# A two-stage linear-attention and gated-MLP layer: reversed layernorm rows on VectorE, contiguous KV copies, reciprocals on either engine, split last tile, new instruction order

## The chip, the cores and the metric

One NeuronCore of a Trainium2 chip. The metric is the device time in microseconds (us) of one execution, the median of several runs. The four runs of the kernel before lie within 0.2% of each other. The five engines run side by side (in the kernel before, TensorE is busy 277.9, VectorE 173.9, ScalarE 154.2 and GpSimd 90.3 us of the same 298.1) and meet at semaphores: TensorE (PE in the profile; its weight loads are PEld), VectorE (DVE), ScalarE (ACT), GpSimd (POOL) and the queue that starts DMA transfers (SP).

## The reference

Input x is 2048 rows of 640 bf16 values. There are two residual stages.

```python
h  = x + A(layernorm(x))          # 32 heads of 20, linear attention
# A: q, k, v = x @ wqkv;  phi(t) = [softmax(t @ w_phi), softmax(-t @ w_phi)]   (per head)
#    kv = phi_k^T v;  z = sum(phi_k);  o = (phi_q kv) / (phi_q z + 1e-6);  return o @ wo
h2 = h + B(layernorm(h))          # B: ((y @ w_gate) * (y @ w_up)) @ w_down,  640 -> 1536 -> 640
```

What matters is the shape of the dependences. Every key row must be projected, exponentiated, summed per head, divided and multiplied into `kv` before the first numerator `phi_q kv` can start. Everything after that can be streamed.

## The kernel before

The kernel records its operations as units and lets a small list scheduler in the same file place them: each unit has a priority (one number per unit, in a list called `ORDER`), a cost, and sometimes a choice of engines (`alts`). The scheduler walks through time and gives each free engine the ready unit of best priority. So a change in one operation's cost or choice of engine can move every instruction of the kernel.

The first stage, per tile of 128 rows: layernorm statistics on VectorE, the normalised row written on ScalarE, a DMA transpose, the V and K projections on TensorE, two exponentials on ScalarE, a sum per head and its reciprocal on VectorE, a multiply on GpSimd, and an accumulation of `kv` on TensorE. The parts that the change touches:

```python
def ln_apply(t, dst):                                   # layernorm row, first stage
    k = xn_p.new()
    R.add("scalar", lambda e: e.activation(out=real(k), in_=x_all[:, t, :], func=ACT.Identity,
                                           bias=mv[:, t, 4:5], scale=mv[:, t, 3:4]), ..., cost=0.92)
    return dma(dst, k, 163840, tr=True)                 # transpose into xnT[:, t, c, :]

def normalise(v, n):                                    # softmax of a key tile, after its exponentials
    sr = sr_p.new()
    R.add("vector", ... tensor_reduce(out=sr[:, 0:n], in_=v, op=ALU.add) ...)
    R.add("vector", ... reciprocal(out=sr[:, 66:66 + n], in_=sr[:, 0:n]) ..., cost=0.56)
    tt("gpsimd", v, v, sr[:, 66:66 + n].unsqueeze(2).to_broadcast([P, n, DH]), ALU.mult)

def kv_evac(c, n):                                      # kv from PSUM to SBUF, masked by g
    ...
    tt("vector", KV[0:kr, c:c + n, HG:HG + DH * nh].rearrange("p c (d h) -> p c h d", d=DH), psv[:, :, :, 0:DH],
       g.unsqueeze(3).to_broadcast([kr, n, nh, DH]), ALU.mult)

def watt(t):                                            # attention output of a tile, second layernorm
    ...
    R.add("scalar", ... activation(out=real(k), in_=h, func=ACT.Identity, bias=nm) ..., cost=0.83,
          alts=[("vector", ... tensor_scalar(out=real(k), in0=h, scalar1=nm, op0=ALU.add) ..., 0.55)])

def fd(t):                                              # last projection of a tile and its store
    pr = psum.new(2)
    ...                                                 # 12 x (512 + 128 columns) of matmul
    R.add("vector", ... scalar_tensor_tensor(out=real(k), in0=real(pr)[:, 0:D], scalar=r2, in1=h, ...) ..., cost=0.88)
    dma(out[0, P * t:P * (t + 1), :], k, 163840, writes=[])
```

The KV copy writes head by head, `d` innermost. In the destination `h` is innermost with six heads, so each element is written six elements (12 bytes) after the last.

The softmax here doesn't subtract the row's maximum and nothing guards it: scores larger than these inputs give would overflow.

## Time and profile before

| | before |
|---|---|
| time, median of 4 runs (range) | 300.24 us (299.85 to 300.54) |
| span of the profiled run | 298.1 us |
| TensorE busy | 277.9 us, 93% |
| first denominator matmul starts | 89.72 us |
| from there to the end | 208.4 us |

The engine line of the page gives busy time, share of the span and number of instructions of each engine.

```profile
...
PE 277.9 (93%) x1969; PEld 163.1 (55%) x2006; DVE 173.9 (58%) x307; ACT 154.2 (52%) x339; POOL 90.3 (30%) x66
...
```

TensorE is the bound: 277.9 of 298.1 us. (37 of its 2006 matmuls are missing from this trace, 1969 against 2006 weight loads; each leaves a false gap of some 0.05 us, 2.0 us in all. Without these gaps TensorE's busy time would be about 279.8.)

The table by stretches cuts the span into pieces. Its columns are the stretch and its length, then busy us and number of instructions of PE, PEld, DVE, ACT and POOL, then the granted TensorE clock as a share of full speed, the busy share of the DMA engines and GB/s.

```profile
...
0.00:20.00 20.00, 13.56 (x110) 9.71 (x113) 14.10 (x35) 13.93 (x25) 14.33 (x34) 1.00 0.73 195
20.00:40.00 20.00, 17.97 (x166) 11.47 (x167) 17.44 (x33) 16.45 (x31) 12.68 (x6) 1.00 0.85 137
40.00:60.00 20.00, 19.79 (x172) 12.31 (x174) 17.17 (x29) 16.53 (x34) 15.47 (x7) 1.00 0.81 181
60.00:80.00 20.00, 17.22 (x155) 10.98 (x157) 15.54 (x19) 13.94 (x28) 18.53 (x8) 1.00 0.84 205
80.00:100.00 20.00, 16.39 (x159) 10.02 (x159) 19.45 (x38) 10.05 (x30) 12.38 (x7) 1.00 0.76 164
...
```

TensorE's idle time is what is left of each 20 us: 6.4, 2.0, 0.2, 2.8 and 3.6 us. Much of the first is the wait for weights (5.3 us, for the DMA of `wqkv`). Between 20 and 80 us VectorE and ScalarE are busy 14 to 17 of 20 us, and GpSimd 18.5 in the last stretch.

The timeline lists instructions in order of time: start, duration, engine, line, operation, output<-input, count, and in brackets the engine's idle time just before, with what ended it.

```profile
...
22.48 2.36 POOL L645 TENSOR_TENSOR r<-r,sr 128x1280 bf16<-128x1280 bf16 x1 [6.26 <-DVE sr L787]
...
81.44 2.36 POOL L645 TENSOR_TENSOR r<-r,sr 128x1280 bf16<-128x1280 bf16 x1 [1.07 <-DVE sr L821]
...
85.89 1.81 DVE L645 TENSOR_TENSOR KV<-ps,G 120x480 bf16<-120x480 f32 x1 [0.55 <-PE ps L628]
...
87.42 1.91 DVE L645 TENSOR_TENSOR KV<-ps,G6d 120x480 bf16<-120x480 f32 x1
...
89.40 0.39 PE L628 MATMUL ps<-pqT,KV 128*128 128x256 bf16 x2 [1.74 <-DVE Zd L891]
...
89.72 1.05 PE L628 MATMUL ps<-pqT,Zd 120*32 120x256 bf16 x22
...
99.97 2.42 POOL L645 TENSOR_TENSOR phq<-phq,sr 128x1320 bf16<-128x1320 bf16 x1 [2.16 <-DVE sr L823]
...
101.13 1.45 DVE L983 TENSOR_SCALAR xn<-x_all,mv 128x640 bf16<-128x640 bf16 x1
...
```

The first key multiply of GpSimd starts at 22.48, after a wait of 6.26 us for a reciprocal of VectorE (line 787). The last one ends at 81.44 + 2.36 = 83.80. The two large KV copies come at 85.89 and 87.42 and take 1.81 and 1.91 us. TensorE waits 1.74 us for the evacuation and starts the first numerator at 89.40 and the first denominator at 89.72. The last two lines are another matter: a VectorE row write (line 983) takes 1.45 us when it starts inside a GpSimd multiply. It ends at 102.58; the multiply ends at 102.39. That row is usually short (a median of 0.386 us), as the groups by shape show (busy time, then mean ns of one, then the idle time before). VectorE:

```profile
...
L983 DVE TENSOR_SCALAR xn<-x_all,mv 128x640 bf16<-128x640 bf16 x6 | 4.3, 720 | 0.1
...
L645 DVE TENSOR_TENSOR KV<-ps,G6d 120x480 bf16<-120x480 f32 x1 | 1.9, 1908 | 0.0
...
L645 DVE TENSOR_TENSOR KV<-ps,G6d 120x120 bf16<-120x120 f32 x1 | 0.7, 662 | 0.0
...
```

The mean of 720 ns for line 983 hides a spread of 286 to 1451 ns. The KV copies are slow for their size: 3.5 ns for each element between the 120- and 480-column forms, (1908 − 662) / 360. ScalarE's row, for comparison:

```profile
...
L748 ACT ACTIVATE xn<-x_all,mv 128x640 bf16<-128x640 bf16 x16 | 14.4, 917 | 3.9 <-DVE mv L743 3.9
...
```

### The profile page before, as it was taken

The page shows a single profiled execution, that of the slowest core. Times are in us where ns is not written, and L with a number is a line of the kernel's source. Part 1 is how long each engine was busy: PE and PEld are TensorE (multiplying, and loading weights), DVE is VectorE, ACT ScalarE, POOL GpSimd, SP SyncE. Part 2 cuts the span into 40 slices and gives each one's busy share as a digit, 9 for nine tenths or more (in the row PEclk, how much of TensorE's full clock was granted, in tenths as well). Part 3 has the DMA queues.
Part 4 walks back from the last instruction along what each step waited for, and adds up shares of the span by engine and source line. Part 5 has one row for each costly group of instructions (what it writes and reads, how often), then busy time and mean ns, then how long its engine had stood idle before and what let it go on. Part 6 is the DMA issues. An engine that isn't in the chain of part 4 may idle for free.

```text
span 298.1 us, 5058 instructions
## 1 busy us (share of the span) xinstructions
PE 277.9 (93%) x1969; PEld 163.1 (55%) x2006; DVE 173.9 (58%) x307; ACT 154.2 (52%) x339; POOL 90.3 (30%) x66
## 2 busy tenths in 40 slices
PE   2899989979868999999999999999999999999995
PEld 2656555645644577666554456564454555444453
DVE  4799696978899965783653544354333316433313
ACT  2998877868338697538633621474251226132200
POOL 7917775998885430333300200000000000000000
PEclk9999999999999999999999999999999999999999
DMA  7788898699692763137330031151001003200001
GB/s 209 190 162 151 134 201 228 91 218 248 185 225 51 134 125 88 35 58 150 90 82 20 0 71 24 46 122 42 1 17 42 28 11 84 83 0 2 0 22 68
DMA packets 60520, 27.86 MB, mean 93 GB/s; under 512 B 49648, under 2 KB 59216, under 8 KB 60496
## 3 DMA queue, kind: packets, MB, share of 16 engines
q1 hardware_dynamic: 60208, 27.20, 40.8%
q8 instruction: 16, 0.26, 0.4%
q10 hardware_dynamic: 288, 0.33, 0.3%
q14 instruction: 8, 0.07, 0.1%
HBM read 12.97 MB, written 2.72 MB: 53 GB/s over the span
## 4 chain that ended last, share of the span: by engine, by line
PE 69%; DVE 17%; POOL 6%; ACT 3%; issue 2%; DMA 1%; SPq 0%; DVEq 0%; ACTq 0%
PE ps L628 68%; DVE sr L785 6%; POOL r L645 5%; DVE sr L821 3%; DVE sr L787 2%; DVE st L735 2%; POOL phq L645 2%; DMA r<-in_A_wqkv_dram 1%; ACT r L639 1%; DVE KV L645 1%; ACT wkv L657 1%; DVE mv L743 1%; DVE r L645 1%; ACT xn L748 1%; DVE sr L823 0%
## 5 line engine op out<-in xcount | busy, mean ns | idle before, releaser
L628 PE MATMUL ps<-xnT,wgu 128*128 128x512 bf16 (+1 forms) x590 | 107.5, 336 | 1.2 <-ACT r L639 0.7
L628 PEld LDWEIGHTS ps<-xnT,wgu 128*128 128x128 bf16 x600 | 58.1, 98 | 47.5 <-ACT r L639 1.0
L639 ACT ACTIVATE r<-ps 128x512 bf16<-128x512 f32 (+2 forms) x92 | 51.8, 574 | 61.7 <-PE ps L628 61.6
L628 PE MATMUL ps<-r 128*128 128x512 bf16 (+6 forms) x612 | 73.1, 270 | 6.4 <-POOL r L645 3.8
L645 DVE TENSOR_TENSOR r<-ps,r 128x512 bf16<-128x512 f32 (+1 forms) x60 | 34.9, 582 | 62.8 <-PE ps L628 51.2
L628 PEld LDWEIGHTS ps<-r 128*128 128x128 bf16 (+2 forms) x620 | 46.1, 109 | 32.1 <-POOL r L645 3.3
L645 POOL TENSOR_TENSOR phq<-phq,sr 128x1320 bf16<-128x1320 bf16 x16 | 38.7, 2424 | 61.4 <-DVE sr L823 56.4
L628 PE MATMUL ps<-wkv,xnT 128*128 128x512 bf16 (+1 forms) x311 | 44.7, 297 | 0.9 <-ACT xn L748 0.4
L645 POOL TENSOR_TENSOR r<-r,sr 128x1280 bf16<-128x1280 bf16 x16 | 37.6, 2357 | 18.2 <-DVE sr L787 12.8
L628 PEld LDWEIGHTS ps<-wkv,xnT 128*128 128x128 bf16 x320 | 24.5, 98 | 18.3 <-issue 0.6
L639 ACT ACTIVATE phq<-ps 128x600 bf16<-128x600 f32 (+1 forms) x64 | 24.8, 446 | 11.1 <-PE ps L628 11.0
L821 DVE TENSOR_REDUCE sr<-phq 128x66 f32<-128x1320 bf16 x16 | 24.0, 1512 | 6.1 <-ACT phq L639 3.5
L628 PE MATMUL ps<-wo,r 128*128 128x128 bf16 (+1 forms) x187 | 27.1, 297 | 0.3
L785 DVE TENSOR_REDUCE sr<-r 128x64 f32<-128x1280 bf16 x16 | 23.3, 1460 | 6.9 <-POOL r L645 5.1
L1017 DVE SCALAR_TENSOR_TENSOR r<-ps,mv,x_all 128x640 bf16<-128x640 f32 x16 | 14.1, 883 | 21.2 <-PE ps L628 21.2
L628 PE MATMUL ps<-wq,xnT 128*128 128x128 bf16 (+1 forms) x156 | 23.6, 297 | 0.2
L982 ACT ACTIVATE xn<-x_all,mv 128x640 bf16<-128x640 bf16 x10 | 8.3, 831 | 28.4 <-DVE mv L650 28.3
L978 DVE SCALAR_TENSOR_TENSOR x_all<-ps,x_all 128x640 bf16<-128x640 f32 x16 | 13.2, 822 | 14.0 <-PE ps L628 14.0
L628 PEld LDWEIGHTS ps<-wo,r 128*128 128x128 bf16 x192 | 14.9, 98 | 10.9
L645 DVE TENSOR_TENSOR r<-ps,rx 128x512 bf16<-128x512 f32 (+1 forms) x30 | 16.5, 570 | 3.6 <-DMA rx<-rows_0 1.5
L628 PEld LDWEIGHTS ps<-wq,xnT 128*128 128x128 bf16 x160 | 12.3, 98 | 8.8 <-ACT r L639 0.3
L639 ACT ACTIVATE lnd<-ps 6x512 f32<-6x512 f32 (+2 forms) x20 | 11.1, 562 | 11.6 <-PE ps L628 11.6
(63 smaller groups left out, 178.9 us busy)
## 6 DMA issues: line engine op xcount, KB each, us to landing
out_dram<-r SPq DMA_DIRECT2D x16, 160.0 KB, 1.8
x_all<-in_A_x_dram SPq DMA_DIRECT2D x7, 320.0 KB, 3.6
wgu<-in_B_w_gate_dram SPq DMA_DIRECT2D x5, 384.0 KB, 4.1
wgu<-in_B_w_up_dram SPq DMA_DIRECT2D x5, 384.0 KB, 4.1
r<-in_B_w_down_dram SPq DMA_DIRECT2D x6, 320.0 KB, 4.7
r<-in_A_wqkv_dram SPq DMA_DIRECT2D x5, 160.0 KB, 4.1
wkv<-in_A_wqkv_dram SPq DMA_DIRECT2D x1, 800.0 KB, 7.0
wo<-in_A_wo_dram SPq DMA_DIRECT2D x5, 150.0 KB
```

What stands on the lines that cost most here:

```text
L628: return R.add("tensor", lambda e: e.matmul(real(o), lhsT=real(l), rhs=real(r), start=start, stop=stop, **kw), [l, r], [o], cost=cost or m ...
L639: return e.activation(out=real(o), in_=real(i), func=func, scale=scale, **kw)
L645: return R.add(eng, lambda e: e.tensor_tensor(out=real(o), in0=real(a), in1=real(b), op=op), [a, b], [o], cost=cost)
L657: alts=[("scalar", lambda e: e.activation(out=real(o), in_=real(i), func=ACT.Copy), 0.17 + n / 1200.0)])
L735: R.add("vector", lambda e, k=k: e.bn_stats(st[:, t, 6 * k:6 * k + 6], x_all[:, t, 320 * k:320 * k + 320]), [x_all[:, t, 320 * k:320 * k + ...
L743: R.add("vector", lambda e: e.scalar_tensor_tensor(out=o, in0=m, scalar=-1.0, in1=r, op0=ALU.mult, op1=ALU.mult), [m, r], [o], cost=0.16)
L785: R.add("vector", lambda e: e.tensor_reduce(out=real(sr)[:, 0:n], in_=real(v), axis=AX.X, op=ALU.add), [v], [sr[:, 0:n]], cost=0.13 + n * ...
L787: R.add("vector", lambda e: e.reciprocal(out=real(sr)[:, 66:66 + n], in_=real(sr)[:, 0:n]), [sr[:, 0:n]], [sr[:, 66:66 + n]], cost=0.56)
L821: R.add("vector", lambda e: e.tensor_reduce(out=real(r4(0)), in_=real(k4), axis=AX.X, op=ALU.add), [k4], [r4(0)], cost=0.13 + n * DH / 960.0)
L978: R.add("vector", lambda e: e.scalar_tensor_tensor(out=h, in0=real(pr)[:, 0:D], scalar=1.0, in1=h, op0=ALU.mult, op1=ALU.add, accum_out=sm ...
L982: R.add("scalar", lambda e: e.activation(out=real(k), in_=h, func=ACT.Identity, bias=nm), [h, nm], [k], cost=0.83, lat=0.08, alts=[("vecto ...
L1017: R.add("vector", lambda e: e.scalar_tensor_tensor(out=real(k), in0=real(pr)[:, 0:D], scalar=r2, in1=h, op0=ALU.mult, op1=ALU.add), [pr[:, ...
```

## The change

Its intent is to unload the key chain. ScalarE's rows may go to VectorE, in a form meant not to collide with GpSimd. VectorE's reciprocals may go to ScalarE as exp(−ln x). The KV copies are written contiguously. The last output tile leaves in two parts, so that the last evacuation is small. The priority list is made anew for all this. The diff, cut to its core:

```diff
+    def turned(t):                       # the row as five chunks of 128, the last chunk first
+        v = x_all[:, t, :]
+        return bass.AP(v.tensor, v.offset + D - P, [list(v.ap[0]), [-P, NC], [1, P]])
     def ln_apply(t, dst):
-        R.add("scalar", ... activation(out=real(k), in_=x_all[:, t, :], ...) ..., cost=0.92)
+        k, x = xn_p.new(), turned(t)
+        R.add("vector", ... tensor_scalar(out=real(k), in0=x, scalar1=mv[:, t, 0:1], scalar2=mv[:, t, 3:4],
+                                          op0=ALU.subtract, op1=ALU.mult) ..., cost=0.46,
+              alts=[("scalar", ... activation(out=<five chunks>, in_=x, ...), 1.0)])
+    def recip(o, i, tmp):
+        def by_ln(e):                    # exp(-ln(x)) on ScalarE, with a semaphore between the two
+            twice[1] += 1
+            e.activation(out=real(tmp), in_=real(i), func=ACT.Ln).then_inc(twice[0], 1)
+            e.wait_ge(*twice)
+            return e.activation(out=real(o), in_=real(tmp), func=ACT.Exp, scale=-1.0)
+        R.add("vector", ... reciprocal(out=real(o), in_=real(i)) ..., cost=0.56, alts=[("scalar", by_ln, 0.72)])
     def proj(pr, t, w):                  # and the same in fu(): chunk c now lies at NC - 1 - c
-            mm(pr[:, 0:512], xnT[:, t, c, :], w[:, c, 0:512], ...)
+            mm(pr[:, 0:512], xnT[:, t, NC - 1 - c, :], w[:, c, 0:512], ...)
     def kv_evac(c, n):
-        tt("vector", KV[...].rearrange("p c (d h) -> p c h d", d=DH), psv[:, :, :, 0:DH], g..., ALU.mult)
+        gd = bass.AP(g.tensor, g.offset, [list(g.ap[0]), [0, n], [0, DH], [1, nh]])
+        tt("vector", KV[...].rearrange("p c (d h) -> p c d h", d=DH),
+           psv[:, :, :, 0:DH].rearrange("p c h d -> p c d h"), gd, ALU.mult)
     def watt(t):
-        R.add("scalar", ... activation(out=real(k), in_=h, ...) ..., cost=0.83, alts=[("vector", ..., 0.55)])
+        x = turned(t)
+        R.add("vector", ... tensor_scalar(out=real(k), in0=x, scalar1=nm, ...) ..., cost=0.46, alts=[("scalar", ..., 0.91)])
     def fd(t):
+        if t == NT - 1:
+            for n0, n1 in ((0, 512), (512, D)):
+                ...                      # all 12 matmuls of this part, then its evacuation and store
+            return
-ORDER = [0 26 5 6 15 1 18 10 ...]        # 1098 priorities
+ORDER = [0 25 10 6 21 14 16 1 ...]       # 1101 priorities
```

Cut here: a change in the scheduler's search for priorities, which a kernel with a full list does not use, the larger scratch tile for `tmp`, one more buffer that the numerator holds, and a cost figure of a weight load.

## The prediction

> **What bounds it now.** The span is 298.1 us and TensorE is busy 277.9 us (93%, engine table) at a granted clock of 1.00, so only idle TensorE is left to win. The busy table by stretches puts it at 6.4 us in 0-20, 2.0 in 20-40, 0.2 in 40-60, 2.8 in 60-80, 3.6 in 80-100, about 2 in 110-295, and 3.2 at the end. So after 100 us only the tail is to be had. Before that, the chain of waits runs through VectorE's head sums and reciprocals and GpSimd's normalisation to the last keys, then the KV evacuation: from 20 to 80 us VectorE is busy 16-17 of every 20 us, ScalarE 14-16.5, GpSimd 13-18.5. GpSimd's last key multiply ends at 83.8 (timeline). From 22.5 to 83.8 it runs 16 key multiplies of 2.36 and 5 query multiplies of 2.42, 49.8 us; the 11 us of gaps are mostly waits for VectorE's reciprocals. TensorE fills in with query projections.
>
> **What changes, costed from the trace.**
> - Layernorm rows: 16 ScalarE passes of 0.917 us become 11 on VectorE and 5 on ScalarE (instruction order). The flat VectorE form takes 0.286 us, but 1.451 once behind a GpSimd multiply. [...]
> - Reciprocals: 18 of 32 leave VectorE (0.546 us each) for two ScalarE passes, estimated 0.5-0.6 us together; in the first 85 us about eight.
> - So before 85 us VectorE is about even, ScalarE does 5 us less.
> - KV evacuation: the 480-column copies take 1.81 and 1.91 us, the 120-column ones 0.53 and 0.66. Contiguous writes should bring them to about 0.65 and 0.28. VectorE saves 3 us, and TensorE's 2.1 us wait before the numerators falls to about 1.
> - Order: three projections (4 us of TensorE filler) move behind the KV evacuation, and 4 query multiplies rather than 5 precede GpSimd's last key multiply. That should end near 78-80 us, and the numerators should start near 81-82 (89.4 now).
> - Tail: last evacuation 0.88 to about 0.35 us, with a smaller last store: −0.5 us.
> - TensorE's work is unchanged.
>
> **Sum.** TensorE idle recovered: start 0.5, 20-80 us about 2.5, evacuation and numerators about 2, tail 0.5: about 5.5 us. Predicted **294.5 us**, 8 in 10 between **290.5 and 298.5**. Chances: faster by over 2% **0.45**, within 2% **0.53**, slower by over 2% **0.02**.
>
> **What would show it.** VectorE's layernorm rows near 0.45 us, none above 1 us under GpSimd; large KV copies under 0.8 us; Ln/Exp pairs near 0.5 us; GpSimd's last key multiply ending before 80; TensorE idle in 20-100 us at 4 us or less against 8.6; TensorE busy still about 277; last evacuation near 0.35. After 100 us, no change beyond 1 us.
>
> **What would make it wrong.** If the reversed form still waits for GpSimd (1 us and more), VectorE gets longer in its busiest stretch and the gain goes. If the write stride was not what made the KV copies slow, 1-2 us are lost. If the first-stage chain hardly shortens, the projections moved behind it no longer fill TensorE and it idles before the numerators: about 298. If the new order fills nearly every gap, the time is about 291. The last tile's 128-column matmuls together may show their weight loads, some tenths.

The 0.45 us under "What would show it" stands as the author's estimate alone. The sum came to 5.5 us off 300.24, but "VectorE is about even" before 85 us rests on that estimate. Other estimates in it name no source, but before's trace has the like: small pairs of ScalarE passes take 291 + 196 ns (128x1) and 311 + 207 (128x2); VectorE's products out of PSUM take 0.691 us at 512 columns and 0.418 at 256, which would be 0.66 at 480 and 0.27 at 120; an evacuation of 640 columns takes 0.883 us, which at that rate would be 0.34 at 128; and a pair of matmuls of 512 and 128 columns takes 0.27 us, five of them 1.4 us for a projection.

## The result, and the profile after

Ratios here are the mean time of one kernel's fast runs over that of the other's of the same rounds, so not quite the ratio of the medians that are quoted.

| | before | after |
|---|---|---|
| time, median (range) | 300.24 us (299.85 to 300.54) | 291.64 us (290.77 to 292.27) |
| ratio, 95% interval | | 0.9712 (0.968 to 0.9745) |
| span of the profiled run | 298.1 us | 289.1 us |
| GpSimd's last key multiply ends | 83.80 us | 76.08 us |
| first denominator matmul starts | 89.72 us | 80.20 us |
| from there to the end | 208.4 us | 208.9 us |

All runs here are fast; the slow one, a longer time at a lower granted TensorE clock, was met once below (even_chunks, 334.03 us at a mean clock of 0.851; in all other runs the mean clock is 0.973 or more). The engine line of after:

```profile
...
PE 278.3 (96%) x2006; PEld 163.3 (56%) x2006; DVE 170.8 (59%) x305; ACT 149.8 (52%) x360; POOL 90.1 (31%) x66
...
```

TensorE's recorded busy time is the same within 0.4 us, or about 1.5 us shorter once the missing records of before are allowed for; the span is 9.0 us shorter. So waits make up about 7.5 of the 9.0 us. The stretches of after, columns as before:

```profile
...
0.00:20.00 20.00, 13.75 (x113) 9.95 (x114) 15.32 (x39) 12.04 (x23) 15.63 (x35) 1.00 0.78 199
20.00:40.00 20.00, 19.07 (x179) 12.35 (x178) 19.19 (x39) 16.71 (x35) 14.96 (x7) 1.00 0.78 146
40.00:60.00 20.00, 20.00 (x172) 12.29 (x171) 18.73 (x27) 16.13 (x40) 15.42 (x7) 1.00 0.78 212
60.00:80.00 20.00, 19.69 (x207) 13.48 (x204) 17.43 (x24) 15.05 (x38) 19.12 (x9) 1.00 0.84 216
80.00:100.00 20.00, 19.43 (x161) 12.50 (x162) 15.51 (x41) 15.20 (x43) 5.60 (x3) 1.00 0.84 146
...
```

TensorE's idle time is now 6.3, 0.9, 0.0, 0.3 and 0.6 us: of the 8.6 us between 20 and 100 us, 1.8 are left. (About 0.6 of the 8.6 are false gaps, of 12 missing records.) The timeline around the KV evacuation:

```profile
...
18.55 2.36 POOL L650 TENSOR_TENSOR r<-r,sr 128x1280 bf16<-128x1280 bf16 x1 [1.14 <-DVE sr L802]
...
69.08 7.00 POOL L650 TENSOR_TENSOR r<-r,sr 128x1280 bf16<-128x1280 bf16 x3
...
76.89 0.66 DVE L650 TENSOR_TENSOR KV<-ps,G6d 120x480 bf16<-120x480 f32 x1 [0.42 <-PE ps L633]
...
79.40 0.66 DVE L650 TENSOR_TENSOR KV<-ps,G 120x480 bf16<-120x480 f32 x1 [1.08 <-PE ps L633]
...
80.20 0.61 PE L633 MATMUL ps<-pqT,Zd 120*32 120x256 bf16 x11 [0.51 <-DVE Zd L912]
...
```

GpSimd's key multiplies start at 18.55, 3.9 us earlier than before. The last three run back to back and end at 69.08 + 7.00 = 76.08. The large KV copies take 0.66 us, or 1.07 ns for each element between the two forms, (657 − 272) / 360, and no longer stand back to back before the denominators, which start at 80.20 after a wait of 0.51 us. VectorE's groups by shape:

```profile
...
L759 DVE TENSOR_SCALAR xn<-x_all,mv 128x640 bf16<-128x640 bf16 x11 | 6.2, 575 | 0.0
L1004 DVE TENSOR_SCALAR xn<-x_all,mv 128x640 bf16<-128x640 bf16 x11 | 6.0, 546 | 0.4
...
L650 DVE TENSOR_TENSOR KV<-ps,G6d 120x480 bf16<-120x480 f32 x1 | 0.7, 657 | 0.4 <-PE ps L633 0.4
...
L650 DVE TENSOR_TENSOR KV<-ps,G6d 120x120 bf16<-120x120 f32 x1 | 0.3, 272 | 0.0
...
```

and ScalarE's:

```profile
...
L761 ACT ACTIVATE xn<-x_all,mv 128x640 bf16<-128x640 bf16 x5 | 4.6, 915 | 0.4 <-DVE mv L748 0.4
...
L801 ACT ACTIVATE sr<-sr 128x66 f32<-128x66 f32 x12 | 3.1, 258 | 0.4
...
L799 ACT ACTIVATE sr<-sr 128x66 f32<-128x66 f32 x12 | 3.1, 255 | 3.7 <-DVE sr L842 3.6
...
```

Eleven of sixteen first-stage rows (line 759) are now on VectorE at 575 ns, between 500 and 605, although GpSimd runs most of that time (46.0 of the first 60 us). The second-stage rows (line 1004) take 546. A reciprocal on ScalarE is 255 + 258 ns. The end of the span:

```profile
...
285.68 1.14 DVE L1036 SCALAR_TENSOR_TENSOR r<-ps,mv,x_all 128x640 bf16<-128x640 f32 x2 [0.20 <-PE ps L633]
```

The two evacuations of the last tile take 1.14 us together, the last one 0.343.

The last row of the table is the main reading. From the first denominator to the end both kernels need the same time within 0.5 us. So nearly the whole gain is that the denominators start 9.5 us earlier, though not all of that is less waiting. Counted in the instruction order, the changed kernel does two query projections fewer before them (80 matmuls against 100), and 6144 matmul columns less in all. In the second stage's streams 49 matmuls of 512 columns take 10.74 us, so 6144 columns are worth about 2.6 us (an estimate). Those 2.6 us are paid after the denominators, and since that part did not get longer, about 2 us of waiting were saved there as well, 0.5 of them in the tail.

### The profile page after: what moved, and what is told of

Its sections match the earlier page's. It is cut to its first block, busy times and chain, and to the rows that moved or that the text cites. A ratio compares the mean times of both kernels' runs of the same rounds, so it can differ in the third digit from the quotient of the medians.

```text
span 289.1 us, 5136 instructions
## 1 busy us (share of the span) xinstructions
PE 278.3 (96%) x2006; PEld 163.3 (56%) x2006; DVE 170.8 (59%) x305; ACT 149.8 (52%) x360; POOL 90.1 (31%) x66
## 4 chain that ended last, share of the span: by engine, by line
PE 85%; DVE 5%; DMA 4%; POOL 2%; SPq 1%; issue 1%; ACT 0%; DVEq 0%
PE ps L633 84%; POOL r L650 2%; DMA r<-in_A_wqkv_dram 2%; DVE sr L807 1%; DMA x_all<-in_A_x_dram 1%; DMA rx<-rows 1%; DVE st L740 1%; PE ps L772 1%; SPq L627 1%; DVE sr L802 1%; DVE sr L842 1%; ACT phq L644 0%; SPq L629 0%; DVE r L650 0%; DVE xn L759 0%
## 5 line engine op out<-in xcount | busy, mean ns | idle before, releaser
L633 PE MATMUL ps<-r 128*128 128x512 bf16 (+6 forms) x620 | 71.2, 272 | 0.9 <-POOL r L650 0.9
L633 PE MATMUL ps<-wkv,xnT 128*128 128x512 bf16 x320 | 45.2, 299 | 0.0
L1036 DVE SCALAR_TENSOR_TENSOR r<-ps,mv,x_all 128x640 bf16<-128x640 f32 (+2 forms) x17 | 14.3, 844 | 31.1 <-PE ps L633 31.0
L633 PE MATMUL ps<-wo,r 128*128 128x512 bf16 x192 | 27.5, 299 | 0.0
L633 PE MATMUL ps<-wq,xnT 128*128 128x512 bf16 (+1 forms) x160 | 24.0, 299 | 0.0
L807 DVE TENSOR_REDUCE sr<-r 128x64 f32<-128x1280 bf16 x16 | 23.3, 1462 | 0.0
L1008 ACT ACTIVATE junk<-x_all,mv 128x640 bf16<-128x640 bf16 x16 | 13.1, 820 | 5.6 <-DVE xn L1004 5.6
```

Of the source, the lines that this page charges most:

```text
L633: return R.add("tensor", lambda e: e.matmul(real(o), lhsT=real(l), rhs=real(r), start=start, stop=stop, **kw), [l, r], [o], cost=cost or m ...
L807: R.add("vector", lambda e: e.tensor_reduce(out=real(sr)[:, 0:n], in_=real(v), axis=AX.X, op=ALU.add), [v], [sr[:, 0:n]], cost=0.13 + n * ...
L1008: R.add("scalar", lambda e: e.activation(out=junk[:, :], in_=h, func=ACT.Square, bias=nm, accum_out=ss), [h, nm], [junk[:, :], ss], cost=0 ...
L1036: R.add("vector", lambda e: e.scalar_tensor_tensor(out=real(o), in0=real(i), scalar=r2, in1=x, op0=ALU.mult, op1=ALU.add), [i, r2, x], [o] ...
```

## The experiments

All twelve runs were on one core against the kernel before on the same chip. "Last key" is the end of GpSimd's last key multiply, "den" the start of the first denominator matmul, "rest" the span from there to the end, all from the profiled run.

| run | what it is | time us | ratio to before (95%) | last key | den | rest |
|---|---|---|---|---|---|---|
| before | | 300.24 | 1 | 83.8 | 89.7 | 208.4 |
| after | | 291.64 | 0.9712 (0.968-0.9745) | 76.1 | 80.2 | 208.9 |
| flat_rows | after, rows flat | 299.58 | 0.9961 (0.9922-1.0) | 84.7 | 89.7 | 209.1 |
| even_chunks | after, ten chunks | 299.78 | 0.9967 (0.9924-1.001) | slow | slow | slow |
| strided_kv | after, KV copy as before | 292.71 | 0.9747 (0.9721-0.9772) | 76.8 | 82.0 | 208.9 |
| recip_vector | after, reciprocals back in place | 295.50 | 0.9838 (0.9813-0.9863) | 80.1 | 83.9 | 209.9 |
| rows_back | after, rows back in place | 295.26 | 0.9838 (0.9785-0.9891) | 80.5 | 84.6 | 208.7 |
| whole_last | after, last tile whole | 292.46 | 0.9729 (0.9688-0.9771) | 76.5 | 80.6 | 209.3 |
| forms_alone | before's order, new operations in place | 297.10 | 0.9881 (0.9831-0.9932) | 82.2 | 86.6 | 209.7 |
| order_alone | after's order, old operations in place | 298.24 | 0.9914 (0.9872-0.9955) | 81.7 | 87.0 | 208.6 |
| kv_alone | before, KV copy contiguous | 298.25 | 0.9925 (0.9877-0.9973) | 84.2 | 88.2 | 208.3 |
| rows_scalar | after, rows as before, placed anew | 310.66 | 1.0329 (1.0281-1.0376) | 84.9 | 99.5 | 209.2 |
| old_order | after with the old priorities, placed anew | 304.29 | 1.0126 (1.0087-1.0165) | 81.8 | 86.3 | 216.4 |
| new_order | before with the new priorities, placed anew | 318.43 | 1.0595 (1.0546-1.0643) | 95.7 | 103.2 | 213.7 |

The rest column is 208 to 210 us in all but old_order, new_order and the slow run. In the others, nearly all of the difference in time is the start of the denominators.

The theory: the new operations shorten the key chain on VectorE and ScalarE, the row form keeps clear of GpSimd, and the order turns that into fewer TensorE waits. The rivals: that the row's form does not matter, only its rate or its engine; that the order alone made the gain; that the KV copies made it.

### flat_rows: does the form of the row matter?

The order on every engine is that of the changed kernel, instruction by instruction. Only the access pattern is different.

```diff
     def turned(t):
-        return bass.AP(v.tensor, v.offset + D - P, [list(v.ap[0]), [-P, NC], [1, P]])
+        return v                          # and xnT / hT read at c again
```

> The changed kernel in its exact order, with only the layernorm rows read as one flat run of 640 columns again instead of five reversed chunks of 128. Theory A (the flat form [...] is kept waiting by GpSimd, and GpSimd by it): of the 11 first-stage rows, those that meet a GpSimd multiply take 1 us or more, the others and the second-stage rows 0.29 us; GpSimd's last key multiply ends 3 us or more later than 76 us; 294 to 298 us. Theory B (only the rate of the row matters, or the order alone made the gain): all rows near 0.3 us, VectorE 3 us freer before 60 us, 290 to 292 us.

Measured: 299.58 us, 0.9961. Nearly all of the gain is gone. The eleven first-stage rows have a median of 657 ns and reach from 342 to 3678. The means of flat_rows by shape:

```profile
...
L759 DVE TENSOR_SCALAR xn<-x_all,mv 128x640 bf16<-128x640 bf16 x11 | 14.0, 1286 | 0.0
...
L1004 DVE TENSOR_SCALAR xn<-x_all,mv 128x640 bf16<-128x640 bf16 x11 | 4.3, 395 | 0.4
...
```

The second-stage rows, written when GpSimd is mostly idle (busy 19.4 of the 120 us from 100 to 220), take 395 ns, faster than the 546 of the changed kernel. The first-stage rows take 1286. The timeline of flat_rows shows why:

```profile
...
11.68 4.26 DVE L759 TENSOR_SCALAR xn<-x_all,mv 128x640 bf16<-128x640 bf16 x2
...
29.96 0.34 DVE L759 TENSOR_SCALAR xn<-x_all,mv 128x640 bf16<-128x640 bf16 x1
...
30.12 2.40 POOL L650 TENSOR_TENSOR r<-r,sr 128x1280 bf16<-128x1280 bf16 x1 [0.56 <-DVE sr L802]
...
30.63 2.08 DVE L759 TENSOR_SCALAR xn<-x_all,mv 128x640 bf16<-128x640 bf16 x1
...
32.62 2.87 DVE L807 TENSOR_REDUCE sr<-r 128x64 f32<-128x1280 bf16 x2
...
```

A row that starts at 29.96, before GpSimd's multiply at 30.12, takes 0.34 us. The next, at 30.63, lies inside the multiply and takes 2.08: it ends at 32.71, 0.19 us after the multiply's end at 32.52, and the key sums behind it (line 807) wait. In total VectorE spends 14.0 us on these rows, 7.8 more than in the changed kernel, and the last key ends 8.6 us later. Theory A holds and theory B falls, except that little is seen of the row keeping GpSimd waiting (that multiply takes 2.40 us, 2.36 is usual). The time is 1.6 us above the upper end that A gave. The form slower by itself is the better one here.

Part of the excess is not at the key multiplies. The first two rows (at 11.68, 4.26 us together) fall into GpSimd's filling of buffers: the first, of 3.68 us, ends at 15.36, just after two such fills in a row (11.20 to 14.50 and 14.44 to 15.18). TensorE then waits 3.2 us for VectorE. Its granted clock falls (0.94 on average over 0 to 20 us, 0.97 over 20 to 40), and until about 21 us a pair of matmuls of 512 and 128 columns takes 0.53 us (the weight loads from 18.31 to 20.98), in the changed kernel 0.27. The first key multiply starts at 23.19 instead of 18.55. So 4.6 of the 8.6 us by which the last key is late are there from the start; the other 4.0 are longer gaps between GpSimd's multiplies.

### even_chunks: the reversal, or the odd number of chunks?

```diff
-        return bass.AP(v.tensor, v.offset + D - P, [list(v.ap[0]), [-P, NC], [1, P]])
+        return bass.AP(v.tensor, v.offset + D - 64, [list(v.ap[0]), [-64, 10], [1, 64]])
```

The halves of each chunk are swapped, so the result is wrong (relative error 0.74). The shapes, sizes and the order are those of the changed kernel.

> Wrong result on purpose: the same reversal with ten chunks of 64 instead of five of 128, all else and the order as in the changed kernel. If it is the odd number of chunks [...], this one behaves like the flat row: about 0.3 to 0.4 us where GpSimd is idle (0.546 with five chunks), over 1 us behind a GpSimd multiply, 294 to 298 us. If it is the chunking or the reversal as such, it takes 0.55 us or more everywhere, no row over 0.8 us, and the time stays within 1 us of 291.6.

Measured: 299.78 us, 0.9967 over its fast runs, 1.8 us above the range given for the odd number of chunks. The profiled execution fell in the slow state (334.03 us, granted clock 0.851 over its whole span), so nothing of TensorE is read from it. VectorE's key sums take 1466 ns in it against 1462 in the changed kernel, so its single instructions may be compared. The second-stage rows have a median of 386 ns, as the flat ones, and the first-stage rows reach 3676. In the timeline of even_chunks:

```profile
...
30.75 2.40 POOL L650 TENSOR_TENSOR r<-r,sr 128x1280 bf16<-128x1280 bf16 x1 [0.56 <-DVE sr L802]
...
31.26 2.08 DVE L759 TENSOR_SCALAR xn<-x_all,mv 128x640 bf16<-128x640 bf16 x1
...
```

The row takes 2.08 us inside a multiply, as in flat_rows. So neither the reversal nor the chunking keeps the row clear of GpSimd: ten reversed chunks collide, five do not. In the changed kernel no row of five takes more than 605 ns; with ten, rows reach 3676. Why the number of chunks decides it is not shown, nor whether it is odd against even: five and ten are the only numbers tried. By the author's argument the reversal has one purpose, to keep the five chunks from being one run. That is not shown either: no run here tried five chunks in ascending order.

### strided_kv and kv_alone: the KV copies

strided_kv is the changed kernel with the copy of before; kv_alone is the kernel before, in its exact order, with the new copy.

```diff
-        tt("vector", KV[...].rearrange("p c (d h) -> p c d h", d=DH),
-           psv[:, :, :, 0:DH].rearrange("p c h d -> p c d h"), gd, ALU.mult)
+        tt("vector", KV[...].rearrange("p c (d h) -> p c h d", d=DH), psv[:, :, :, 0:DH], g..., ALU.mult)
```

> The changed kernel with only the KV evacuation written head by head with a step of six again. If the evacuation lies on the path to the numerators: large copies 1.8 to 1.9 us, small ones 0.5 to 0.7, first denominator matmul 1.3 to 2.5 us later than 80.2, 293 to 294 us. If it is covered by other work: within 0.5 us of 291.6.

Measured: 292.71 us, 0.9747. The ratio is 0.0035 above that of after, about 1.1 us; the two intervals overlap, so the times alone do not show it. It is just below the 293 to 294 us expected. The timeline of strided_kv has the copies and the denominators:

```profile
...
77.58 1.81 DVE L650 TENSOR_TENSOR KV<-ps,G6d 120x480 bf16<-120x480 f32 x1 [0.41 <-PE ps L633]
...
82.01 0.61 PE L633 MATMUL ps<-pqT,Zd 120*32 120x256 bf16 x11 [1.32 <-DVE Zd L911]
...
```

The denominators start 1.8 us later, at 82.01 (1.3 to 2.5 were expected), after a wait of 1.32 us instead of 0.51. So the copies are on the path, but in the new order one of them is done while TensorE still has projections to do.

> The kernel before in its exact order with only the KV copies made contiguous. If they lie on its path to the numerators: large copies 0.66 us, numerators 1.5 to 3 us earlier than 89.4, 297 to 299 us. If not: 300.

Measured: 298.25 us, 0.9925, or 2.3 us off the kernel before; the denominators start 1.5 us earlier. By the ratios the contiguous form is worth 2.3 us in the old order and 1.1 in the new one, but each figure has an error of over 1 us, and the denominators move by 1.5 and 1.8 us. So no difference between the two orders is shown. Neither is it shown which part of the edit made the copies fast: the new form writes without steps, but it also reads PSUM with a step of 21 elements and the mask `g` with a step of one in place of the same element again and again, and no run separates these.

### recip_vector: the reciprocals

The order of all other instructions is that of the changed kernel. After the scheduler has placed everything, the 18 pairs on ScalarE are put back as one VectorE reciprocal each, at the same place.

```diff
             u.at, u.end, u.eng = at[u], ends[u], eng[u]
+            if u.alts[0][2] == 0.56:      # a reciprocal
+                u.eng = "vector"
```

> The changed kernel in its exact order, with the 18 reciprocal pairs of ScalarE put back as one VectorE reciprocal each at the same place in the order. If VectorE's load holds up the keys: about eight more of 0.55 us before 80 us, so GpSimd's last key multiply ends 2 to 4 us later than 76 us, 293 to 295.5 us. If the order made the gain and the engine of the reciprocal does not matter: within 1 us of 291.6.

Measured: 295.50 us, 0.9838, so 3.8 us over after. The last key ends at 80.10, 4.0 us later. The stretches of recip_vector:

```profile
...
20.00:40.00 20.00, 17.48 (x165) 11.22 (x164) 19.96 (x34) 13.75 (x25) 12.49 (x6) 1.00 0.67 127
40.00:60.00 20.00, 19.97 (x169) 11.93 (x167) 19.97 (x34) 14.09 (x31) 13.32 (x6) 1.00 0.68 170
...
```

VectorE is busy 19.96 and 19.97 of 20 us: it is full there, and the reciprocals of 0.55 us that are put back there lengthen the chain.

### rows_scalar and rows_back: ScalarE's rows

rows_scalar puts the rows back as they were, flat and with ScalarE as first choice, and lets the scheduler place everything anew. rows_back puts them back at their places in the changed kernel's order (17 go to ScalarE, one to VectorE).

```diff
 rows_back:
             u.at, u.end, u.eng = at[u], ends[u], eng[u]
+            if u.n in [<the rows that had been on ScalarE>]:
+                u.eng = "scalar"          # flat pattern; TensorE reads chunk c at c again
```

> The changed kernel with only the layernorm rows as before: flat, on ScalarE in the first stage, on either engine in the second; the scheduler places them anew from the same priorities. If moving the rows off ScalarE [...] is the main part: 294 to 297 us, ScalarE busy over 17.5 of every 20 us between 20 and 80. If the rest of the change carries it: 291 to 293 us.

Measured: 310.66 us, 1.0329, 10 us worse than before. That was outside both expectations. ScalarE was busy 14.4 to 16.3 of 20 us between 20 and 80, not over 17.5. The timeline of rows_scalar shows a TensorE that stood still for 7.35 us:

```profile
...
98.78 0.40 PE L633 MATMUL ps<-pqT,KV 128*128 128x256 bf16 x1 [7.35 <-ACT phq L644]
...
```

So the new placing, not ScalarE's load, made this run slow. The trace shows the wait before it: ScalarE's query exponentials (line 644) stood still for 6.76 us until 96.56, for the DMA transposes of the query tiles, behind four query multiplies of GpSimd that ended at 94.45.

> The changed kernel in its exact order, with only the rows put back as before in place (17 move to ScalarE, one to VectorE, flat). If ScalarE's load in the first stage is what the rows cost: 11 rows of 0.92 us more before 60 us, where ScalarE is busy 16 of 20 us, last key multiply 4 to 8 us later than 76 us, 295 to 300 us. If the slow rows_scalar run came of its new placing and not of the rows: within 2 us of 291.6.

Measured: 295.26 us, 0.9838, or 3.8 us over after. The stretches of rows_back:

```profile
...
20.00:40.00 20.00, 18.04 (x168) 11.53 (x166) 17.59 (x28) 17.07 (x33) 13.46 (x6) 1.00 0.69 138
40.00:60.00 20.00, 18.41 (x151) 10.99 (x152) 16.53 (x27) 19.00 (x44) 13.32 (x6) 1.00 0.69 172
...
```

ScalarE is busy 17.1 and 19.0 us here, against 16.7 and 16.1 in the changed kernel, and the last key ends 4.4 us later. So the rows' engine is worth about 4 us. The other 15 us between the two runs came from the placing, not from the rows.

### old_order and new_order: priorities exchanged

```diff
 old_order:  the changed operations
-ORDER = [0 25 10 6 ...]
+ORDER = [0 26 5 6 ...]                  # last tile's entries spread over its two parts
 new_order:  the old operations, with the new list
```

> The changed operations with the old list of priorities (the last tile's entries spread over its two parts). If the cheaper operations made the gain: 292 to 295 us, the first denominator matmul at 81 to 84 us. If the new order made it: 297 to 300 us.

> The kernel before, operations untouched, with the new list of priorities (the last tile's two parts joined). If the cheaper operations made the gain: 297 to 300 us, TensorE idle again 5 us or more between 20 and 100 us. If the new order made it: 292 to 294.5 us.

Measured: 304.29 us (1.0126) and 318.43 us (1.0595). Both are slower than the kernel before and outside what either theory gave, the second far outside. As an experiment on the split they failed: a list of priorities is not an order. The scheduler turns it into one by way of costs and choices of engine, and with other costs it makes another order, tuned to nothing. Neither kernel has the TensorE order of before or of after. With operations for which it was not made, neither list was worth anything. The question of the split was put again with the orders themselves.

### forms_alone and order_alone: the split

```diff
 forms_alone:  before, placed by its own costs and list; then, unit by unit
+            if u.n in [<rows that are on VectorE after>]:        put the reversed VectorE form in
+            if u.n in [<reciprocals that are on ScalarE after>]: put exp(-ln x) in
+ ... and the contiguous KV copies
 order_alone:  after, placed by its own costs and list; then
+            rows flat and on the engines of before, reciprocals on VectorE, strided KV copies
```

> The kernel before in its exact order on TensorE, GpSimd and the queue, with the new operations put in place of the old ones: the same rows go to VectorE in reversed chunks and the same 18 reciprocals to ScalarE as in the changed kernel, and the KV copies are contiguous. The two runs with swapped priority lists let the scheduler place everything anew with a list tuned to other operations and were both slow, so they don't split the gain; this one and the next do. If the operations by themselves carry it: 293 to 296 us. If they only pay once the order is made for them: 297 to 300 us. A waiting order that they upset: over 300.

> The changed kernel in its exact order, with the operations of before put in place: flat rows on the engines they had, all reciprocals on VectorE, strided KV copies (only the split last tile stays). If the order by itself carries the gain: 292 to 296 us. If the order needs the new operations: ScalarE takes 17 rows more of 0.9 us and VectorE about eight reciprocals more in the first stage, GpSimd's last key multiply ends after 84 us, 299 to 310 us.

Measured: 297.10 us (0.9881) and 298.24 us (0.9914). From the ratios, on 300.2 us, the operations by themselves give 3.6 us, the order by itself 2.6, and both together 8.6. About 2.5 us exist only when both are there. The intervals are about 1 to 1.5 us wide to each side, so this last figure is not much more than its error. (A small difference blurs it: order_alone has the split tail, forms_alone does not.) The third outcome, that one of them carries it, is ruled out: neither 0.9881 nor 0.9914 is near 0.9712. order_alone met neither of its ranges (292 to 296, 299 to 310), and its last key ends at 81.74, not after 84.

GpSimd's part of the traces shows where the two meet. Its time up to the last key is the start of the first key multiply, the multiplies themselves (16 for keys, and those for queries that come before the last key) and the gaps between them.

| | first key multiply starts | query multiplies before the last key | gaps | last key ends |
|---|---|---|---|---|
| before | 22.48 us | 5 | 11.5 us | 83.80 us |
| forms_alone | 22.92 us | 5 | 9.5 us | 82.22 us |
| order_alone | 18.89 us | 4 | 15.5 us | 81.74 us |
| after | 18.55 us | 4 | 10.1 us | 76.08 us |

Of the 7.7 us by which the last key ends earlier, 3.9 are the earlier start, 2.4 one query multiply fewer and 1.4 shorter gaps. The first two come with the order, even with the old operations. In before VectorE starts the first tile's sum at 16.33 but its reciprocal only at 21.90, after another tile's sum and statistics; in after the sum starts at 16.40 and the reciprocal at 17.92. But in the new order the old operations let the gaps grow to 15.5 us. The new operations shorten them by 2.0 us in the old order and by 5.4 in the new one: that is the part that needs both, in these profiled runs.

forms_alone also shows what may be a cost that a count of waits misses, in TensorE's clock. In its profiled run, by stretches:

```profile
...
28.00:32.00 4.00, 2.51 (x36) 2.01 (x34) 4.00 (x8) 2.98 (x5) 1.96 (x1) 1.00 0.58 120
32.00:36.00 4.00, 3.55 (x17) 1.93 (x18) 3.45 (x10) 1.56 (x4) 2.71 (x2) 0.61 0.55 132
...
```

Between 28 and 36 us TensorE was short of work (it waited 1.93 us for a key multiply, until 32.45), and after that the granted clock, in the column before the last two, was down to 0.61 on average over 32 to 36 us, and 0.96 over the next four. While it is down TensorE works at about half its pace: between 33.48 and 35.61 a pair of matmuls of 512 and 128 columns takes 0.53 us (by its weight loads in the timeline), in the changed kernel 0.27. The two of its four runs with a mean clock of 0.999 took 296.1 and 296.3 us, and the two with 0.993 and 0.994 took 297.9 and 298.0. Such a dip need not cost anything: in recip_vector three runs with 0.994 took 295.1 to 295.7 us and the one with 0.999 took 295.6. The drop is plainer in rows_scalar after its 7.35 us of standstill:

```profile
...
92.00:96.00 4.00, 0.00 (x0) 0.00 (x0) 0.00 (x0) 0.00 (x0) 2.44 (x2) 0.86 1.26 201
96.00:100.00 4.00, 0.85 (x13) 0.47 (x17) 1.24 (x1) 2.85 (x8) 0.00 (x0) 0.50 1.17 227
100.00:104.00 4.00, 3.78 (x30) 2.39 (x23) 3.75 (x8) 2.93 (x9) 3.05 (x2) 0.50 0.18 34
...
```

TensorE stops at 91.43 and starts again at 98.78. The clock is at 0.50 from 96 to 104; the means of 0.86 on both sides put its fall at about 94.9, some 3.5 us after the stop, and its return at about 105.1 (an estimate, with the clock either 1.00 or 0.50 there). In forms_alone the wait before the drop was only 1.93 us, and before has a wait of 1.86 us (at 60.9) with the clock at 1.00 throughout, so neither what sets off a drop nor what ends it is shown. In both runs the low clock went on when TensorE had work again: for some 6 us in rows_scalar, at least until 35.6 in forms_alone. The changed kernel's profiled run stays at 1.00 through all stretches up to 280 us.

### whole_last: the tail

```diff
-        if t == NT - 1: ...               # two parts
+        # the last tile like every other
```

> The changed kernel with the last output tile evacuated and stored whole again. From the end of the last matmul to the end of the span 0.4 to 0.6 us more than in the changed kernel, last evacuation 0.88 us instead of 0.34; 291.9 to 292.3 us. If the weight loads of the 128-column matmuls ate the gain: no difference, 291.6.

Measured: 292.46 us, 0.9729 with an interval from 0.9688 to 0.9771; one of its six runs took 295.05. The difference from after is within the noise of the times. The traces are clearer. The last line of whole_last's timeline:

```profile
...
286.70 0.88 DVE L1043 SCALAR_TENSOR_TENSOR r<-ps,mv,x_all 128x640 bf16<-128x640 f32 x1 [0.20 <-PE ps L640]
```

From the end of the last matmul to the end of the span it has 3.2 us (286.66 to 289.9), the changed kernel 2.7 (286.31 to 289.05). The split is worth 0.5 us, as the shorter last evacuation would have it. From the end of the last evacuation to the end of the span they have 2.3 and 2.2 us, so the smaller store is hardly faster.

## Why the prediction was right, and where not

The prediction was 294.5 us with a range of 290.5 to 298.5; measured were 291.64. The direction, the mechanism and the range held, though it had given "within 2%" the larger chance (0.53) and the result is 2.9% faster. The size was 5.5 us where 8.6 came. Point by point:

- **TensorE's idle time before 100 us is what there is to win.** Right: busy time stayed at 278 us, and the denominators' start carries the result.
- **The flat row collides with GpSimd and the new form does not ("none above 1 us under GpSimd").** Right, and shown by flat_rows (342 to 3678 ns in the first stage) against after (500 to 605). The reason given for it is not shown. It was undervalued: with this one thing undone, 7.5 us of the gain go (0.9961 against 0.9712).
- **Rows "near 0.45 us".** Wrong: 0.575 in the first stage, 0.546 in the second. The 0.45 lies 0.164 above the fastest of the six flat rows, 0.286. Their median, and that of the second-stage rows of flat_rows, is 0.386. Measured, the new form costs 0.160 more than that (0.546 against 0.386), so the step was right and the start was not.
- **Ln/Exp pairs at 0.5 to 0.6 us, about eight in the first 85 us.** Right: 0.513; but eleven of them come that early.
- **VectorE about even, ScalarE 5 us less before the numerators.** Roughly: up to the denominators VectorE had 2.6 us less (70.8 against 73.4) and ScalarE 3.6 less (60.1 against 63.7).
- **KV copies at 0.65 and 0.28.** Right: 0.66 and 0.27.
- **"Three projections (4 us of TensorE filler) move".** Miscounted: two, worth about 2.6 us.
- **Last key at 78-80 us, numerators at 81-82.** Too late: 76.08, and 79.2 for the first numerator. The query multiply fewer was foreseen; that GpSimd's key multiplies would start 3.9 us earlier was not.
- **Tail −0.5 us.** Right: 0.5. The weight loads of the last tile's 128-column matmuls did not show: in the changed kernel the last 12 start 56 ns apart, and where such matmuls alternate with those of 512 columns the next one also starts 56 ns after them.
- **After 100 us, no change beyond 1 us.** Right as far as the traces tell. Their idle time there differs by about 1.9 us, but about 1.2 of them are the false gaps of missing matmul records; kv_alone, with the same TensorE order and all 2006 records, shows 0.7 us.

The term of the sum that was mis-sized is the idle time recovered in the first stage and at the evacuation: "20-80 us about 2.5, evacuation and numerators about 2". In the tables by stretches it went from 5.0 to 1.2 us in 20-80 and from 3.6 to 0.6 in 80-100, so 6.8 instead of 4.5, or about 6.2 without the false gaps of before. (The term "start 0.5" gave 0.2.) That is the case that the prediction had set aside with "if the new order fills nearly every gap, the time is about 291". The estimate treated the engines' savings and the new order as separate small gains and gave the order little. What the order did that the estimate lacks is to start the key multiplies 3.9 us earlier, with the old operations too (order_alone). And forms_alone and order_alone suggest that the gains are not separate: 3.6 and 2.6 us alone, 8.6 together, with GpSimd's gaps shortened by 2.0 us in the old order and by 5.4 in the new.

What stays open: which single waits make up the gaps that shorten only when both are there. The part of TensorE's clock in it (the two runs of forms_alone with the lower mean clock took 1.8 us longer) was seen, but not varied by itself.

No run beat the changed kernel, and the experiments point to none that would: of its 10.8 us of idle TensorE, 6.3 lie in the first 20 us, 6.2 of them waits for the first weights, and 2.7 in the tail.

## What to carry to other kernels

Where GpSimd is busy, choose VectorE's access patterns by whether they collide with it, not by their speed alone: here the form that is slower when alone (0.55 against 0.39 us) was worth 7.5 us. Make the order for the operations and the operations for the order, and compare parts of a change at a fixed order; a list of priorities given to other operations measures something else. And take the median of an instruction's durations, not the best, when it is to stand for the next one.
